# The streamed first weight read through ScalarE's queue instead of SyncE's, and placed behind the fold's first copy in the joint sweep

## The chip, the cores and the metric

One core of a Trainium2 chip runs the whole program in one launch. The metric is device time in microseconds (us) for one execution. TensorE (PE) multiplies, VectorE (DVE) and ScalarE (ACT) do the element work, GpSimd (POOL) does a little of it, and SyncE (SP) only issues transfers. A transfer can be issued by more than one engine: each has a queue of its own, and an engine issues in program order, so an instruction that waits holds everything behind it in that engine's queue.

## The reference

Eight heads of attention with 32 packed positions, then a mix over the sequence, then a mix over channels:

```python
p_packed = sm_attn(p, k, v)              # (8, 8, 32, 64)
out = sm_attn(q, p_packed, p_packed)     # (8, 8, 576, 64)
x = out.transpose(0, 2, 1, 3).reshape(8, 576, 512)
u = x + (x.transpose(0, 2, 1) @ U @ V).transpose(0, 2, 1)
result = u + np.maximum(u @ w_ch1, 0.0) @ w_ch2   # w_ch1 512x2048, w_ch2 2048x512
```

`sm_attn` scales, subtracts the row maximum, exponentiates, divides by the sum, and multiplies with the values. All data are float32.

## The kernel before, in words

**The fold.** The output of attention is a weighted sum of 32 packed rows, so `u @ w_ch1` need not be multiplied with the whole 512 rows of the weight for every position. For each batch the kernel first multiplies the packed rows with the weight. This is the fold: `fold_products` (L556 to 563) takes a quarter of the columns of `w_ch1`, a tile of 128 x 2048 float32 (1 MB), and writes two PSUM banks with eight matmuls (L562, `t_ps`). `folded` (L565 to 576) then splits each bank into a high half, copied by ScalarE (L574, `wth`), and a low half, the difference, made by VectorE (L576, `wtl`). There are four casts of each kind per quarter. A float32 product is then three matmuls: high with high, low with high, high with low (L100, L101, L102 into `h_ps`).

**The quarters.** The four quarters c = 0 to 3 are folded once for each of the eight batches. For the first two batches they lie on chip as `w1t[c]`; while they are there, each is also saved to DRAM (`save_w1`, L549, tensor `w1D`). From then on the room is wanted for other tiles, and each quarter is read back from `w1D` when it is needed, into one tile `w1s` with a single buffer (`stream_w1`, L552 to 554). So a read of the next quarter cannot start before the eight matmuls of the quarter before have read the tile, and the next eight matmuls cannot start before the read has landed. There are 24 such reads: two in the loop of the second batch (at `kt` 10 and 14, L1275 to 1278), and the rest in the six late batches.

**The rest.** Each half of a first product leaves PSUM through ScalarE (`leave`, L1034: into `bits`, `ppall` and others; `last1`, L801: into `aP`). The second product with `w_ch2` is done by sweeps over eight turns (`Sweep.turn`, L1085, into four banks `o`), with seven products in place of eight for a 2 x 2 block, so sums of operands are formed first by VectorE (L1046 to 1048), split high by ScalarE (L1069) and low by VectorE (L1074). Of the sums of `w_ch2` some are brought from DRAM, 256 KB at a time (`bring`, L952, `tc<-tD`). Part of the hidden values of each batch is held out to DRAM (L1037, `hD`; L979, `hjD`) and read back later. Each batch's packed rows are loaded by L958 and L966, the queries by L290, the packed values for the fold by L137, and results are stored by L849.

**The order.** Nothing is scheduled by the hardware or by a planner: the order of instructions on each engine is the order in which the Python program calls them, and that is written out by hand as strings of short words. `run` (L1392 to 1406) goes through the words; each names a list of calls in the table `stages` (L1349 to 1388) and takes the next call from it. `batch_steps` holds one late batch, `joint_steps` (L1315 to 1319) what follows the first four batches, and `last_steps` the end. The words that matter here, with or without a closing `n`, `j` or `J`: `F0` the fold's eight matmuls, `F1` one high cast, `F2` one low cast, `S` one call of `stream_w1`, `H` one half of a first product, `E` the eviction of a half, `L` a cast of `last1`, `G` products of a sweep's turn, `C` and `D` the high and low split, `P` one `bring`, `W` one store of held-out values, `M` and `N` emptying and combining the sums of a sweep, `O` a store of results, `Y` and `Z` the save and the reload of rows.

In `batch_steps` every `S` already stands directly behind the first `F1` after its `F0`, or some words later; in `joint_steps` the one `Sn` stands near the end of the second line, after `Wn G`. `joint_steps` is run once, behind batch 3.

**Semaphores.** The program's transfers signal their landing on a small set of semaphores that are used in turn, and a later transfer on the same semaphore waits for the earlier one.

Of the kernel before, what the change touches and what calls it, by code (L numbers as in the profile page):

```python
# [20 lines left out]
def packed_attention_mixer_kernel(  # L21
# [27 lines left out]
    nc = tc.nc  # L49
    B, H, S, D = q.shape  # L50
# [20 lines left out]
    U, V, w1, w2 = (a.bitcast(I32) for a in (U, V, w1, w2))  # L71
# [53 lines left out]
    w1D = [dram.tile([P, 4 * QW], F32, name=f"w1D{c}", tag=f"w1D{c}") for c in range(NPC)]  # L125
# [425 lines left out]

    def stream_w1(c):  # L552
        t = w1t["s"] = pipe.tile([P, 4, QW], F32, name="w1s", tag=f"w1t{NPC - 1}", bufs=1)
        nc.sync.dma_start(out=t.rearrange("p x n -> p (x n)"), in_=w1D[c])

    def fold_products(b, c):  # L556
        f_ps = [bank() for _ in range(2)]
# [702 lines left out]
    for kt in range(NK):  # L1260
# [11 lines left out]
        if kt % 4 == 2:  # L1272
            n = NPC + kt // 4 + 1
            fold(n // NPC, n % NPC)
            if kt == 10:  # L1275
                stream_w1(0)
            if kt == 14:
                stream_w1(1)
# [8 lines left out]
        c, y = divmod(kt - 1, 2)  # L1287
# [26 lines left out]
    )  # L1314
    joint_steps = (  # L1315
# [3 lines left out]
    )  # L1319

# [55 lines left out]
    for x in ("", "n"):  # L1376
        stages.update({
            "H" + x: [lambda h=h: h[0].half(*h[1:]) for h in halves[x]],
            "E" + x: [lambda h=h: h[0].leave(*h[1:]) for h in halves[x]],
            "L" + x: [lambda h=h: h[0].now.last1(2 * h[1] + h[2]) for h in halves[x] if not h[0].r and h[2] < 2],  # L1380
            "W" + x: [lambda h=h: h[0].hold_out(h[1]) for h in halves[x] if h[2] == 3],
            "F0" + x: [lambda f=f: fold_one(NPC * f[0] + f[1]) for f in folds[x]],
            "F1" + x: [lambda f=f, m=m: folded_one(4 * (NPC * f[0] + f[1]) + m, False) for f in folds[x] for m in range(4)],
            "F2" + x: [lambda f=f, m=m: folded_one(4 * (NPC * f[0] + f[1]) + m, True) for f in folds[x] for m in range(4)],
            "S" + x: [lambda f=f: stream_w1((f[1] + 1) % NPC) for f in folds[x] if f != (B - 1, 3)],
        })
# [52 lines left out]
```

## Time and profile before

| | us |
|---|---|
| median of 3 runs (764.04, 764.5, 764.6) | 764.5 |
| profiled execution, its own time | 765.2 |
| span of the profiled execution | 763.2 |
| TensorE busy in the span | 749.9 |
| VectorE busy | 587.5 |
| ScalarE busy | 405.7 |
| GpSimd busy | 84.9 |

The granted clock of TensorE is 1.0, the upper of its two levels, over the whole span. The profile is one execution, read with its own span as the measure; the median of the other runs is 0.7 us below its own time.

In the rows below a line such as L562 is a line of the kernel, `t_ps<-w1s,ppT` says which tile is written from which, and x16 means sixteen instructions in a row taken together. A bracket at the end of a timeline's row gives the idle time of the engine just before it and what ended it. `SPq` and `ACTq` are the sequencers of SyncE and ScalarE, which issue transfers; the duration of a transfer's row there is that of the issue, not of the transfer. In a chain of waits a row that begins with DMA is the transfer itself, from issue to landing.

### The profile page before, as it was taken

How to read it: one execution, taken by the hardware profiler on the slowest of the kernel's cores; microseconds unless marked ns; L12 is line 12 of the kernel's file. 1: busy time of each engine (PE TensorE's matmuls, PEld its weight loads, DVE VectorE, ACT ScalarE, POOL GpSimd, SP SyncE). 2: the span in 40 equal slices, each digit the busy share in tenths (PEclk: the TensorE clock that was granted, in tenths of full speed). 3: DMA queues.
4: the chain of work that ended last, by engine and by line, in shares of the span. 5: the costliest groups of instructions: out<-in, count | busy, mean ns of one | idle time of the engine just before them, and what ended most of it. 6: DMA issues, size and time to landing. Idle time of an engine off the chain costs nothing.

```text
span 763.2 us, 19553 instructions
## 1 busy us (share of the span) xinstructions
PE 749.9 (98%) x7795; PEld 662.2 (87%) x7795; DVE 587.5 (77%) x1216; ACT 405.7 (53%) x1018; POOL 84.9 (11%) x116
## 2 busy tenths in 40 slices
PE   8999999999999999999999999999999999999997
PEld 6667787887878889998999989999999989999997
DVE  4799789976787768867888768867887678764876
ACT  4788765554343645555455544555554554555451
POOL 1123111010111002100201002010201020200000
PEclk9999999999999999999999999999999999999999
DMA  9999984369112874656478474657464746463672
GB/s 318 337 355 305 324 219 157 112 228 300 40 42 88 254 250 140 221 195 200 130 229 267 132 245 148 185 168 244 145 192 166 253 126 202 148 239 125 198 224 105
DMA packets 106090, 151.78 MB, mean 199 GB/s; under 512 B 40464, under 2 KB 60176, under 8 KB 102416
## 3 DMA queue, kind: packets, MB, share of 16 engines
q1 hardware_dynamic: 105856, 150.28, 61.6%
q8 instruction: 62, 1.02, 0.5%
q14 instruction: 28, 0.23, 0.1%
q10 hardware_dynamic: 144, 0.26, 0.1%
HBM read 116.56 MB, written 33.95 MB: 197 GB/s over the span
## 4 chain that ended last, share of the span: by engine, by line
PE 85%; DMA 6%; DVE 4%; ACT 3%; issue 1%; SPq 0%; POOL 0%; ACTq 0%
PE o L1085 33%; PE h_ps L100 9%; PE h_ps L101 8%; PE h_ps L102 8%; PE t_ps L562 4%; PE o L100 3%; PE o L101 3%; PE o L102 3%; DMA w1s<-w1D 2%; DMA kx<-in_k_dram 2%; PE t_ps L301 1%; PE o L1114 1%; PE s_ps L321 1%; PE t_ps L321 1%; PE m_ps L696 1%
## 5 line engine op out<-in xcount | busy, mean ns | idle before, releaser
L1085 PE MATMUL o<-w2h,h 128*128 128x256 f32 x832 | 166.9, 281 | 0.0
L100 PE MATMUL h_ps<-ah,wth 128*128 128x256 f32 (+1 forms) x512 | 157.5, 308 | 0.6 <-ACT hj L801 0.3
L101 PE MATMUL h_ps<-al,wth 128*128 128x256 f32 (+1 forms) x512 | 150.4, 294 | 0.0
L102 PE MATMUL h_ps<-ah,wtl 128*128 128x256 f32 (+1 forms) x512 | 150.3, 294 | 0.0
L1085 PEld LDWEIGHTS o<-w2h,h 128*128 128x128 f32 x832 | 136.2, 189 | 2.6 <-issue 2.6
L1074 DVE TENSOR_TENSOR h<-bits,h 128x896 fp32r<-128x896 f32 (+1 forms) x104 | 107.8, 1037 | 31.2 <-ACT h L1069 30.5
L1069 ACT CAST h<-bits 128x896 fp32r<-128x896 f32 (+1 forms) x104 | 93.7, 901 | 58.0 <-DVE bits L1048 39.7
L100 PEld LDWEIGHTS h_ps<-ah,wth 128*128 128x128 f32 x512 | 96.4, 188 | 25.2 <-ACT ppall L1034 8.4
L1085 PE MATMUL o<-w2l,h 128*128 128x256 f32 x416 | 116.0, 279 | 0.0
L101 PEld LDWEIGHTS h_ps<-al,wth 128*128 128x128 f32 x512 | 96.3, 188 | 1.0
L102 PEld LDWEIGHTS h_ps<-ah,wtl 128*128 128x128 f32 x512 | 96.3, 188 | 0.0
L1034 ACT ACTIVATE bits<-h_ps 128x256 f32<-128x256 f32 x132 | 49.5, 385 | 67.4 <-PE h_ps L102 51.5
L1085 PE MATMUL o<-tb,h 128*128 128x256 f32 x468 | 81.2, 282 | 0.1
L1085 PEld LDWEIGHTS o<-w2l,h 128*128 128x128 f32 x416 | 78.1, 188 | 0.0
L576 DVE TENSOR_TENSOR wtl<-t_ps,wth 128x256 fp32r<-128x256 f32 x128 | 49.4, 417 | 29.4 <-ACT wth L574 28.3
L1085 PEld LDWEIGHTS o<-tb,h 128*128 128x128 f32 x468 | 66.7, 189 | 0.6 <-DVE h L1074 0.3
L1046 DVE TENSOR_TENSOR bits<-bits 128x256 f32<-128x256 f32 x96 | 42.9, 447 | 28.6 <-ACT bits L1034 28.4
L574 ACT CAST wth<-t_ps 128x256 fp32r<-128x256 f32 x128 | 42.6, 376 | 27.0 <-PE t_ps L562 20.4
L452 POOL TENSOR_TENSOR al<-aT,ah 128x320 fp32r<-128x320 f32 (+1 forms) x32 | 31.4, 985 | 207.0 <-ACT ah L448 178.4
L100 PE MATMUL o<-w2h,h 128*128 128x512 f32 x128 | 52.1, 407 | 0.0
L101 PE MATMUL o<-w2l,h 128*128 128x512 f32 x128 | 50.6, 395 | 0.0
L102 PE MATMUL o<-w2h,h 128*128 128x512 f32 x128 | 50.5, 395 | 0.0
(212 smaller groups left out, 1379.8 us busy)
## 6 DMA issues: line engine op xcount, KB each, us to landing
w1s<-w1D SPq DMA_DIRECT2D x24, 1024.0 KB, 5.5
tc<-tD SPq DMA_DIRECT2D x94, 256.0 KB, 3.1
bits<-in_moe_w_ch_dram SPq DMA_DIRECT2D x32, 512.0 KB, 4.6
kx<-in_k_dram SPq DMA_DIRECT2D x16, 576.0 KB, 5.9
x<-in_q_dram SPq DMA_DIRECT2D x16, 576.0 KB, 5.9
out_dram<-os SPq DMA_DIRECT2D x33, 256.0 KB, 2.9
vt<-in_v_dram SPq DMA_DIRECT2D x32, 256.0 KB, 6.1
hD<-ppall SPq DMA_DIRECT2D x30, 256.0 KB, 4.1
```

The costliest lines, as they stand in the source:

```text
L100: nc.tensor.matmul(ps, lhsT=lh, rhs=rh, start=start, stop=False)
L101: nc.tensor.matmul(ps, lhsT=lh, rhs=rl, start=False, stop=False)
L102: nc.tensor.matmul(ps, lhsT=ll, rhs=rh, start=False, stop=stop)
L452: nc.gpsimd.tensor_tensor(al, aT[:, ns], ah.bitcast(F32), op=ALU.subtract)
L562: nc.tensor.matmul(f_ps[g][xs], lhsT=ppT[b][zs, g, xs], rhs=w[zs, h // 2], start=True, stop=True)
L574: nc.scalar.copy(hi[:, g], src)
L576: nc.vector.tensor_tensor(lo[:, g], src, hi[:, g].bitcast(F32), op=ALU.subtract)
L1034: nc.scalar.activation(dst[:, 256 * (i % 2):256 * (i % 2) + 256], src, AF.Relu)
L1046: vec(l[:, 4:6], s[:, 1:3], s[:, 0:1].to_broadcast([P, 2, P]), op=ALU.add)
L1069: nc.scalar.copy(h[:, ks], src)
L1074: nc.vector.tensor_tensor(lo[:, ks], src, h[:, ks].bitcast(F32), op=ALU.subtract)
L1085: nc.tensor.matmul(ps, lhsT=a, rhs=b, start=x not in self.begun, stop=last and i == 2)
```

## The change

Two edits. `stream_w1` issues its transfer on ScalarE's queue instead of SyncE's, in all of its 24 calls; and in `joint_steps` the word `Sn` moves from behind `Wn G` to directly behind the first `F1n`, so that there too the read stands right after the fold's first high cast. Nothing is computed differently, and no transfer is added or left out.

```diff
     def stream_w1(c):
         t = w1t["s"] = pipe.tile([P, 4, QW], F32, name="w1s", tag=f"w1t{NPC - 1}", bufs=1)
-        nc.sync.dma_start(out=t.rearrange("p x n -> p (x n)"), in_=w1D[c])
+        nc.scalar.dma_start(out=t.rearrange("p x n -> p (x n)"), in_=w1D[c])
@@ joint_steps
-        "Ln PJ D G F0n C N A N N D G O G G U En F1n G F1n G C G G En U Hn N Hn En N Hn D O En Pn Hn Ln Pn En Wn G Sn "
+        "Ln PJ D G F0n C N A N N D G O G G U En F1n Sn G F1n G C G G En U Hn N Hn En N Hn D O En Pn Hn Ln Pn En Wn G "
         "G C G Mv F1n G D En Ln M G Yn M Zn U Hn M F2n Hn En F2n F2n En F1n F2n Wn "
```

## Rows read from the trace of the kernel before

**Rows 1.** The page, part 1: busy time, share of the span, instructions.
```profile
PE 749.9 (98%) x7795; PEld 662.2 (87%) x7795; DVE 587.5 (77%) x1216; ACT 405.7 (53%) x1018; POOL 84.9 (11%) x116
```
**Rows 2.** TensorE's waits: line, releaser, us in total, times, longest.
```profile
PE t_ps L562 <- DMA w1s<-w1D: 1.4, 2, 0.9
```
**Rows 3.** TensorE's timeline: start, us, instruction, idle before and what ended it.
```profile
279.89 1.09 PE L562 MATMUL t_ps<-w1s,ppT 64*32 64x512 f32 x16 [0.92 <-DMA w1s<-w1D]
...
446.21 1.09 PE L562 MATMUL t_ps<-w1s,ppT 64*32 64x512 f32 x16 [0.49 <-DMA w1s<-w1D]
```
**Rows 4.** The page, parts 3 and 6: queues; issues with KB, median us to landing.
```profile
q10 hardware_dynamic: 144, 0.26, 0.1%
...
w1s<-w1D SPq DMA_DIRECT2D x24, 1024.0 KB, 5.5
tc<-tD SPq DMA_DIRECT2D x94, 256.0 KB, 3.1
```
**Rows 5.** Chains of waits, from 268 to 282 and 430 to 448 us.
```profile
273.39 6.37 DMA w1s<-w1D
...
437.31 8.76 DMA w1s<-w1D
```
**Rows 6.** ScalarE's timeline, 267 to 277 us.
```profile
269.15 0.65 ACT L574 CAST wth<-t_ps 128x256 fp32r<-128x256 f32 x2 [0.64 <-PE t_ps L562]
...
271.56 0.67 ACT L1034 ACTIVATE bits<-h_ps 128x256 f32<-128x256 f32 x2
...
274.92 0.38 ACT L1034 ACTIVATE ppall<-h_ps 128x256 f32<-128x256 f32 x1 [2.57 <-PE h_ps L102]
```
**Rows 7.** SyncE's timeline, 335 to 346 us, and its waits (as rows 2).
```profile
335.70 0.46 SPq L554 DMA_DIRECT2D w1s<-w1D  x1
...
339.49 5.51 SPq L966 DMA_DIRECT2D ppP<-ppD  x4
...
SPq L966 <- DMA w1s<-w1D: 12.7, 5, 3.0
```
**Rows 8.** Line 958 around 266.8 us: issues with durations in ns; landing times.
```profile
L958 SPq DMA_DIRECT2D aP<-aD x2: 486/830/1175, 265.6 to 266.8; - x2
...
DMA to landing us min/median/max: 5.0/5.6/6.1
```
**Rows 9.** TensorE's timeline, 273 to 275 us.
```profile
273.95 0.37 PE L100 MATMUL h_ps<-ah,wth 128*128 128x256 f32 x1
```
**Rows 10.** Timelines of SyncE, 425 to 440 us, and ScalarE, 427 to 432 us.
```profile
426.14 7.91 SPq L849 DMA_DIRECT2D out_dram<-os  x2
...
427.63 0.64 ACT L574 CAST wth<-t_ps 128x256 fp32r<-128x256 f32 x2
430.26 0.52 ACT L1069 CAST h<-aJ 128x384 fp32r<-128x384 f32 x1 [2.00 <-PE o L1085]
```
**Rows 11.** Line 554: its issues, ns min/median/max, first and last start.
```profile
L554 SPq DMA_DIRECT2D w1s<-w1D x24: 320/424/715, 226.3 to 681.6; - x24
```
**Rows 12.** Line 1069's wait (ns, as rows 11) and ScalarE's timeline there.
```profile
L1069 ACTq EVENT_SEMAPHORE  x1: 1672/1672/1672, 317.0 to 317.0; - x1
...
317.02 0.66 ACT L1034 ACTIVATE bits<-h_ps 128x256 f32<-128x256 f32 x2 [0.26 <-DVE h L1074]
```
**Rows 13.** Line 952 at 317.1: issue, landing; TensorE's timeline where it is used.
```profile
L952 SPq DMA_DIRECT2D tc<-tD x1: 537/537/537, 317.1 to 317.1; - x1
...
DMA to landing us min/median/max: 2.8/2.8/2.8
...
321.62 0.52 PE L1085 MATMUL o<-tc,h 128*128 128x256 f32 x3
```
**Rows 14.** ScalarE's timeline, 315 to 318.5 us.
```profile
315.76 0.64 ACT L574 CAST wth<-t_ps 128x256 fp32r<-128x256 f32 x2
```
**Rows 15.** Chains of waits, 329 to 333 and 506 to 510 us: TensorE's products.
```profile
329.75 3.07 PE o L1085 x27
...
506.66 3.18 PE o L1085 x27
```

## The prediction

> **What bounds the kernel now.** I read the page first: TensorE is busy for 98% of the span [rows 1], so only time in which it stands still, or is made to stand still, can change the end. Next, whom TensorE waited for: behind the opening stages two of its waits are worth naming, and both are for the streamed first weight, 1.4 us together, the longest 0.9 [rows 2]. Its timeline shows where: the fold's products at 279.89 stood 0.92 us and those at 446.21 stood 0.49 us, each released by the read's landing [rows 3]. The reads themselves are 1 MB each, 24 of them, median 5.5 us from issue to landing, and all of them leave through SyncE's queue, in line with 94 reads of 256 KB (L952) and the rest; ScalarE's queue carried 0.26 MB in the whole run [rows 4]. So what the change can give directly is those two waits, 0.92 + 0.49 = 1.4 us, which is 0.18%. I count 0.2%, 1.5 us, as about what a measurement of this kernel tells from no change.
>
> The profiled execution took 765.2 us, 2.0 more than its span of 763.2, and lies 0.7 above the median of 764.5. The sum is made on the span, and its difference is carried to the median.
>
> **Part 1: the read behind the products at 279.89.** The chain of waits from 268 to 282 us goes from ScalarE through SyncE's store and its save of hidden rows (L979, 272.69) to the read at 273.39, which lands 6.37 later [rows 5]. On ScalarE's queue the read stands directly behind its cast at 269.15 [rows 6], so it no longer waits for that save. But it cannot leave at once. SyncE's queue shows that a transfer waits for the landing of the one eight places ahead: the four reads at 339.49 take 5.51 us to issue because the third of them stands eight behind the weight's read at 335.70 (one L1037 and four L958 lie between), and L966 waits for that read in five places, 12.7 us in total [rows 7]. I take this counter to be common to both queues, since the trace has only the one transfer on ScalarE's and can't show it. Eight ahead of the read at 273.39 (one L979, two L849, four L966 between) is the last L958, the second of a pair issued at 265.6 and 266.8; their landing times are 5.0 and 6.1 us [rows 8]. Taking the shorter for the later one, it lands at about 266.8 + 5.0 = 271.8. The read then leaves at 271.9, not 273.39: 1.5 us earlier, more than the 0.92 that TensorE waited. Gain: 0.9 us.
>
> The price is that ScalarE stands still from 269.2 to 271.9 with the read at its head, 2.3 us or so beyond the 0.2 to 0.4 it has free. Queued behind it are the fold's three other casts, the cast for VectorE's low part and the evictions L1034 at 271.56. ScalarE has 2.57 us idle before 274.92 [rows 6], so it catches up, but TensorE needs the banks those evictions free for its next half at 273.95 [rows 9]. The two evictions end at 272.24; 2.3 later is 274.5, so TensorE stands up to 0.6 us; if the first eviction alone decides, about 0.3. Bounds 0 and 0.8; I take 0.4, between these.
>
> **Part 2: the joint sweep's read.** SyncE issued it at 437.31 [rows 5] behind two stores that held the queue from 426.14 for 7.91 us; ScalarE does the fold's first copies at 427.63 [rows 10] and then has 2.00 us idle, so the issue costs nothing there. The read leaves some 9 us earlier and is down long before TensorE came for it at 446.21 - 0.49 = 445.7 [rows 3], even if it takes the 8.8 us that it took. Gain: 0.5 us. Nothing is next late: the products are then ready 9 us ahead.
>
> **Part 3: the 22 other issues on ScalarE.** One such issue took 320 to 715 ns on SyncE, median 424 [rows 11]. The read's own wait, for the fold's products, has ended when ScalarE gets there: the cast in front of it waited for them. I cost them at nothing, because the queue works ahead of the engine: a wait of L1069 that belongs to the next instruction begins at 317.0 and lasts 1.67 us, while the engine is executing the eviction that began at 317.02 [rows 12]. An issue of 0.42 that starts with a cast of 0.38 leaves a hole of about 0.1. If that cover fails, each read pushes ScalarE by 0.42, 10.1 us in 24; ScalarE has gaps of 0.2 to 2 us every few instructions, so nearly all of it is taken up, and I bound it by one place per batch that has none: 6 x 0.42 = 2.5 us. From below a gain is excluded, as nothing is taken off ScalarE.
>
> **Part 4: the transfers that no longer stand in one line.** SyncE's queue loses 24 issues (10 us) and 25 us of waiting in front of them, so that what stands behind the reads leaves earlier; TensorE waits for none of that. But what stands ahead of them may now be met by them. In five sweeps the read L952 of 256 KB is the last transfer before the weight's read. At 317.1 it lands 2.8 us later, at 319.9, and TensorE uses it at 321.62: 1.7 us to spare [rows 13]. ScalarE reaches its place with the casts at 315.76 [rows 14], so the 1 MB read would go out ahead. The difference of the median landings, 5.5 - 3.1 = 2.4 us [rows 4], is what the small one can lose by it. The other four, by the same three rows of each: 1.8 to spare at 655.11, 0.3 at 498.62 (there it took 5.0 us), and 2.4 at two more. At a full 2.4 that is 0.7 + 0.6 + 2.1 + 0 + 0 = 3.4 us; at none it is 0. No row of this trace shows two busy queues beside each other. I take 0.6, one of the two middling places, since the transfers' sum of bytes is the same and the read needs its own microsecond to begin.
>
> First what the row shows: the read at 273.39 landed after 6.37 us in a queue that still held stores [rows 5]. The Trainium skill, "DMA: Bandwidth & Descriptors", section "Queues, rings and completion order", says that SyncE and ScalarE each own a row and that every DMA engine goes round among the rows that have work, packet by packet. By that rule the weight's read overtakes the queue, which is the slower rival below. The same page, "Issuing engines are not separate DMA queues", adds that issuing from two engines saves only the issuer's time; by it the sum would be without Part 1's gain.
>
> **Sum.** -0.9 + 0.4 - 0.5 + 0 + 0.6 = -0.4: 764.5 - 0.4 = **764.1 us**. TensorE's own pace is left as it is, and adds to the range: 27 products of L1085 took 3.07 us at 329.75 and 3.18 at 506.66 [rows 15] at the same granted clock, and which of the two holds changes at places I can't predict; but whole batches differ by only some 0.15, so I allow 0.6 either way.
>
> **Rivals.**
> - *Faster: both waits go and nothing comes back.* Parts 1's price and 4 at zero: -1.4, and with the pace in favour -2.0: 762.5. For it: the small reads of Part 4 lie in gaps of 1.7 and more. Against: ScalarE's stop at 269 is in the order of the transfers.
> - *Slower: the 1 MB read overtakes the small one.* As Part 4 at its full price: -0.9 + 0.4 - 0.5 + 3.4 = +2.4: 766.9. It decides from a delay of 1.7 us on. For it: ScalarE does get there first at 317 and 650. Against: only three places are tight. The Trainium skill's round among the rows, cited above, is on its side.
> - *Slower: the issue isn't covered on ScalarE.* -0.4 + 2.5 = +2.1: 766.6.
> - *The change moves nothing.* If the read at 269 leaves ScalarE no earlier than SyncE sent it, Part 1 is only price: +0.4 - 0.5 + 0.6: 765.0, within 0.2%.
>
> **How the numbers follow.** Forecast 0.48, nothing moved 0.08, faster 0.20, overtaken 0.17, not covered 0.07. So within 0.2% 0.56, faster 0.20, slower 0.24. The range goes from the faster rival, which has the pace in its favour, 762.5, to the overtaken one with the pace against it, 766.9 + 0.6 = 767.5; about one in ten is left out on each side.
>
> **What would show it.** Right: TensorE's waits for w1s gone from the list; a ScalarE idle of about 2.3 us near 269.5, and none like it elsewhere; ScalarE's queue carrying 24 MB and the joint's read leaving near 428. Wrong: waits of TensorE for tc near 321, 498 and 655 (overtaken); gaps of 0.4 us on ScalarE behind each read, with TensorE waiting for h_ps (not covered); the read near 272 not leaving before 273 (nothing moved). Above all a common counter that holds ScalarE in more places than the one at 269 would make the forecast too low.

## The result

The changed kernel took 773.6 us (median of four runs, 771.4 to 774.6) against 764.3 us (median of four runs): slower by 1.2%, a ratio of 1.0118 with a 95% interval of 1.0095 to 1.0140, or some 9 us. The forecast was 764.1, and the range ended at 767.5.

The page of the changed kernel, parts 1, 3 and 6, answers to [rows 1] and [rows 4]:

```profile
span 771.1 us, 19564 instructions
...
PE 751.9 (98%) x7795; PEld 661.8 (86%) x7795; DVE 588.7 (76%) x1216; ACT 406.5 (53%) x1018; POOL 84.6 (11%) x116
...
q1 hardware_dynamic: 102400, 125.11, 51.4%
q10 hardware_dynamic: 3600, 25.43, 9.6%
...
w1s<-w1D ACTq DMA_DIRECT2D x24, 1024.0 KB, 5.7
tc<-tD SPq DMA_DIRECT2D x94, 256.0 KB, 2.9
```

25 MB have gone from the first queue to the second, as intended. The median landings have hardly moved (5.7 for 5.5, 2.9 for 3.1), and TensorE's busy time is 2 us longer; neither row gives away 9 us. TensorE's waits do (columns as in [rows 2]):

```profile
PE o L1085 <- DMA tc<-tD: 3.4, 3, 1.3
...
PE t_ps L301 <- DMA x<-in_q_dram: 1.3, 1, 1.3
PE t_ps L562 <- DMA w1s<-w1D: 1.3, 1, 1.3
```

Before, the last of these came to 1.4 in two places ([rows 2]), and the other two were not among the waits of 0.2 us or more. Where they are, by TensorE's timeline; the second and the fourth row answer to [rows 3], the third to [rows 13]:

```profile
271.43 1.09 PE L562 MATMUL t_ps<-w1s,ppT 64*32 64x512 f32 x16 [1.31 <-DMA w1s<-w1D]
282.32 1.09 PE L562 MATMUL t_ps<-w1s,ppT 64*32 64x512 f32 x16
325.16 0.62 PE L1085 MATMUL o<-tc,h 128*128 128x256 f32 x3 [1.00 <-DMA tc<-tD]
449.93 1.09 PE L562 MATMUL t_ps<-w1s,ppT 64*32 64x512 f32 x16
503.66 0.61 PE L1085 MATMUL o<-tc,h 128*128 128x256 f32 x3 [1.06 <-DMA tc<-tD]
526.38 0.63 PE L301 MATMUL t_ps<-ident,x 128*128 128x128 f32 x4 [1.33 <-DMA x<-in_q_dram]
663.13 0.62 PE L1085 MATMUL o<-tc,h 128*128 128x256 f32 x3 [1.34 <-DMA tc<-tD]
```

Both old waits are gone, and five new ones have come, all for transfers. TensorE's instructions are the same 7795 in the same order in both kernels, so each can be set beside its counterpart by number. The steps by which the changed kernel (called after from here on) falls behind at one instruction are, in us: 1.4 at 271, then -1.0 at 282, 1.1 at 325, -0.6 at 450, 1.3 at 504, 1.5 at 526, 1.6 at 663. Two more parts are small: 0.9 between 230 and 265 us, and 0.6 in many little ones. From 230 to 700 us that is 6.8. Another 1.1 has gathered by 140 us, ahead of the first streamed read, where nothing was edited, and the tail adds nothing: 7.9, the difference of the two spans.

What happened to a transfer, by line, beside its counterpart. First the `tc` read at 319.3 in after ([rows 13] has it before, 2.8 us to landing):

```profile
L952 SPq DMA_DIRECT2D tc<-tD x1: 536/536/536, 319.3 to 319.3; - x1
...
  PE o L1085: 1.0, 1
...
DMA to landing us min/median/max: 5.8/5.8/5.8
```

Then the queries' read (L290) of before, at 511.6, and of after, at 516.8:

```profile
L290 SPq DMA_DIRECT2D x<-in_q_dram x1: 551/551/551, 511.6 to 511.6; - x1
...
DMA to landing us min/median/max: 6.0/6.0/6.0
```

```profile
L290 SPq DMA_DIRECT2D x<-in_q_dram x1: 583/583/583, 516.8 to 516.8; - x1
...
DMA to landing us min/median/max: 9.4/9.4/9.4
```

And the weight's third read, at 262.6 in after; before, at 260.7, it took 6.0 us:

```profile
L554 ACTq DMA_DIRECT2D w1s<-w1D x1: 327/327/327, 262.6 to 262.6; - x1
...
  PE t_ps L562: 1.3, 1
...
DMA to landing us min/median/max: 8.7/8.7/8.7
```

So the damage runs both ways: small transfers beside the read land 1.5 to 3.4 us later, and the read itself is stretched by 2.7 us, with a store of SyncE's (L849, at 262.87) just behind it. How the two queues share the engines is seen from 500 to 502 us of after, while the `tc` read issued at 497.1 is still out. The view of the transfers has queue, pieces (packets in the view), MB and share of 16 engines:

```profile
q10 hardware_dynamic: 89, 0.72, 90.4%
q1 hardware_dynamic: 11, 0.02, 3.5%
```

In these 2 us the weight's queue moved 89 pieces of 8 KB and SyncE's queue 11 small ones. One piece of the weight costs 0.904 x 16 x 2 / 89 = 0.325 us of an engine. Its 128 pieces are 8 to an engine if they are spread evenly, so by this estimate an engine that has turned to the weight is away for about 8 x 0.325 = 2.6 us, and a `tc` read with a few pieces left on such an engine waits for it. No view names the engine of a piece, so this is worked out and not seen. The Trainium skill, "DMA: Bandwidth & Descriptors", section "Queues, rings and completion order", states that an engine drains a whole packet, typically 9 to 17 descriptors, from one queue before it goes on to the next. The trace agrees as far as it goes: 89 pieces of the weight pass with 11 small ones among them; where a packet ends no view shows.

### The profile page after: what moved, and what is told of

Read it like the earlier page. It is cut to its first block, busy times and chain, and to the rows that moved or that the text cites. A ratio compares the mean times of both kernels' runs of the same rounds, so it can differ in the third digit from the quotient of the medians.

```text
span 771.1 us, 19564 instructions
## 1 busy us (share of the span) xinstructions
PE 751.9 (98%) x7795; PEld 661.8 (86%) x7795; DVE 588.7 (76%) x1216; ACT 406.5 (53%) x1018; POOL 84.6 (11%) x116
## 4 chain that ended last, share of the span: by engine, by line
PE 76%; DMA 10%; DVE 7%; ACT 4%; issue 1%; SPq 1%; POOL 0%; ACTq 0%; DVEq 0%
PE o L1085 30%; PE h_ps L100 8%; PE h_ps L101 7%; PE h_ps L102 7%; PE t_ps L562 4%; DMA bits<-in_moe_w_ch_dram 3%; PE o L100 3%; PE o L101 3%; PE o L102 3%; DMA tc<-tD 2%; PE t_ps L301 1%; DMA kx<-in_k_dram 1%; PE o L1114 1%; DMA x<-in_q_dram 1%; PE t_ps L321 1%
```

## Experiments

Two theories were set against each other. A: the two queues share the 16 transfer engines, so that what used to be served in order of issue is now served side by side, and what TensorE needs first lands late. B: ScalarE, standing at 24 issues and at their semaphores, holds up the evictions. The ratio is to executions of the kernel before that were measured alongside; their medians were 765.6 to 766.1 us, so that times which an expectation counts from 764.3 lie some 1.5 us low. "230 to 700" is how much longer TensorE took from the instruction that the first trace of before ran at 230.2 us to the one that it ran at 700.1, worked out from one timeline each; it leaves out the opening, which is in no kernel's edits and varied by 0 to 2.2 us.

| run | ratio, 95% interval | 230 to 700, us |
|---|---|---|
| before, three traces | | 0, -1.3, -0.6 |
| after, three traces | 1.0118 (1.0095 to 1.0140) | +6.8, +7.9, +8.6 |
| e1_move_only | 0.9998 (0.9985 to 1.0010) | -0.2 |
| e2_queue_only | 1.0119 (1.0096 to 1.0141) | +8.6 |
| e3_two_on_act | 1.0008 (0.9996 to 1.0019) | -1.1 |
| e4_19_on_act | 1.0034 (1.0011 to 1.0057) | +1.5 |
| e5_small_on_act | 0.9998 (0.9986 to 1.0010) | -0.7 |
| e6_2kb_pieces | 1.0053 (1.0032 to 1.0073) | +1.4 |
| e7_gpsimd | 1.0060 (1.0040 to 1.0080) | +4.4 |
| e8_five_on_act | 1.0093 (1.0063 to 1.0123) | +3.0 |
| e10_2kb_one_queue | 1.0013 (1.0003 to 1.0022) | -0.2 |
| e11_later | 1.0125 (1.0075 to 1.0176) | +9.5 |
| f1_behind_casts, two traces | 1.0032 (1.0013 to 1.0052) | -0.5, +0.9 |
| f2_both_behind, two traces | 1.0004 (0.9987 to 1.0021) | -1.3, +2.5 |

### The two parts alone

e1_move_only keeps `nc.sync` and moves the word; e2_queue_only keeps the word's place and changes the queue.

```diff
-... U En F1n G F1n G C ... Wn G Sn "
+... U En F1n Sn G F1n G C ... Wn G "
```

> Only the joint sweep's one read is moved behind the fold's first copy; all 24 reads stay on SyncE's queue. Theory A (two queues share the transfer engines, so the 1 MB reads stretch the small transfers and are stretched by them): with one queue nothing is shared, so only the 0.5 us wait at 446 goes: 763.8, between 763.4 and 764.5. Rival B (the loss is ScalarE standing at its issues and their semaphores): the same. Rival C (the moved word itself costs, since the read now stands ahead of two stores): over 766.

> All 24 reads on ScalarE's queue, the joint sweep's word left where it was. Theory A: as the changed kernel plus the 0.5 us wait at 446 that comes back, 774, between 772.5 and 775.5, with TensorE waiting for tc near 324, 503 and 663 and for the queries near 526. Rival B: the same time. Rival C: near 765.

The move costs nothing, and the queue makes the whole loss. In e2 the expected wait at 446 did not come back, although the read stood at its old place; the row answers to the second of [rows 3]:

```profile
452.02 1.09 PE L562 MATMUL t_ps<-w1s,ppT 64*32 64x512 f32 x16
```

So theory A's figure for that wait was wrong in e2. Its absence there says little of the edit: further down, two of three traces of the kernel before do not have the wait either.

### Some reads on ScalarE's queue, some on SyncE's

`stream_w1` counts its calls and takes ScalarE's queue for some of them; the word is moved in all three kernels.

```diff
+    reads = []
 ...
+        reads.append(c)
+        queue = nc.scalar if len(reads) - 1 in (3, 10) else nc.sync
-        nc.sync.dma_start(...)
+        queue.dma_start(...)
```

> Only the reads behind the two waits of before (the 4th, near 272, and the joint sweep's, the 11th) go through ScalarE's queue, the others through SyncE's; the joint word is moved. Theory A: both waits go and no tight transfer is met: 764.3 - 0.9 - 0.5 = 762.9, between 762.3 and 763.9. Rival B: ScalarE stands for a semaphore at the 4th read and costs 0.4 or more there: 763.3 to 764.3.

> As the changed kernel, but the five reads next to which TensorE's new waits stand (the 3rd, 6th, 14th, 15th and 22nd, at 263, 319, 498, 516 and 657 us of after) go back to SyncE's queue; 19 stay on ScalarE's. Theory A: the new waits of 1.4, 1.1, 1.3, 1.5 and 1.6 us go, 6.9 together: 773.6 - 6.9 = 766.7, between 765 and 768. Rival B (cost by the number of issues on ScalarE): 19/24 of the loss stays, 764.3 + 7.4 = 771.7.

> Only the five reads of the fourth experiment's list (3rd, 6th, 14th, 15th, 22nd) go through ScalarE's queue, the other 19 through SyncE's, joint word moved. Theory A: behind the opening the five bring the 5.4 us that the fourth experiment took away, less the joint's 0.5: 764.3 + 4.9 = 769.2, between 768 and 771, with waits for tc at 324, 503 and 663. Rival B (by the number of issues): 5/24 of 9 us: 766.2.

The five reads that stand beside the new waits carry the loss: without them 19 issues on ScalarE cost 2.6 us (e4), with them alone it is 7.1 us (e8). By number of issues it would have been the other way round. The 7.1 us are more than the 4.9 that theory A gave, and no trace shows them in full: the one execution that was profiled is, with 769.5 us, the shortest of e8's five, and the three longest had a lower mean granted clock (0.995 to 0.998, against 1.0). Its waits:

```profile
PE t_ps L566 <- DMA w1s<-w1D: 2.1, 1, 2.1
PE o L1089 <- DMA tc<-tD: 1.6, 4, 0.7
```

e3 is level with before and not 1.4 us better. It does show ScalarE's stop at the common semaphores, as Part 1 foretold, on ScalarE's timeline (`ACTq` is its queue's issue; two added lines shift the numbers by 4):

```profile
271.10 0.37 ACT L578 CAST wth<-t_ps 128x256 fp32r<-128x256 f32 x1 [0.64 <-PE t_ps L566]
273.54 0.35 ACTq L558 DMA_DIRECT2D w1s<-w1D  x1
273.94 0.65 ACT L578 CAST wth<-t_ps 128x256 fp32r<-128x256 f32 x2 [2.46 <-DMA ppP<-ppD]
```

ScalarE stands for 2.46 us at a transfer of SyncE's queue. Then TensorE's timeline of e3:

```profile
276.46 0.39 PE L100 MATMUL h_ps<-ah,wth 128*128 128x256 f32 x1
```

TensorE ran this matmul at 273.95 before ([rows 9]); in e3 it was 1.95 us behind up to 273, and is 2.5 behind here. So the stop cost TensorE 0.6 us. e4 has the same stop: ScalarE stood 3.02 us until 274.01, and TensorE fell 1.1 us behind there, a good part of what e4 still loses. In the changed kernel the same place cost nothing: TensorE had been held up by the read ahead, the semaphores had come free, and ScalarE stood for 0.33 us.

### Issues without bytes

e5_small_on_act leaves the 24 reads on SyncE's queue, with the word moved, and lets ScalarE issue a transfer of 64 bytes at each of the 24 places.

```diff
+    spot = dram.tile([1, 16], F32, name="spot")
         nc.sync.dma_start(out=t.rearrange("p x n -> p (x n)"), in_=w1D[c])
+        nc.scalar.dma_start(out=spot, in_=w1D[c][:1, :16])
```

> All 24 reads stay on SyncE's queue (joint word moved); at each of the 24 places ScalarE's queue issues in addition one transfer of 64 bytes from the weight to a spare place in DRAM, which takes part in the round of semaphores and moves next to no bytes. Theory A (shared transfer engines): nothing of the loss comes, apart from ScalarE's stop at the 4th place, 0.5 us: 764 to 765.5, no new waits of TensorE for tc. Rival B (ScalarE's issues and semaphore waits): most of the 9 us comes: 769 to 773.

The small transfers by their line (durations in ns, first and last start):

```profile
L557 ACTq DMA_DIRECT2D spot<-w1D x24: 475/475/561, 228.8 to 682.4; - x24
```

24 issues of 0.475 us each on ScalarE, in the same round of semaphores, cost nothing: 0.9998. ScalarE did stand 1.74 us here at the 4th place, until 272.9, and TensorE lost nothing by it; in the changed kernel it stood for no more than 0.33 us behind any of its 24 reads. So theory B falls as the cause of the loss, though a stop at a semaphore can cost something, as e3 and e4 show.

### The size of a piece

e6_2kb_pieces lays the saved weight out in DRAM so that a read goes in pieces of 2 KB; e10_2kb_one_queue does the same on SyncE's queue.

```diff
-    w1D = [dram.tile([P, 4 * QW], ...
+    w1D = [dram.tile([4 * P, QW], ...
 ...  (save_w1 likewise)
-        nc.scalar.dma_start(out=t.rearrange("p x n -> p (x n)"), in_=w1D[c])
+        nc.scalar.dma_start(out=t, in_=w1D[c].rearrange("(x p) n -> p x n", p=P))
```

> As the changed kernel, but the saved weight lies in DRAM so that each read (and each of the four saves) goes in pieces of 2 KB instead of 8 KB; bytes, queue and places are the same. Theory A1 (the engines serve the two queues piece by piece, so a queue with 8 KB pieces gets four times the share of one with 2 KB pieces): TensorE's waits for tc near 324, 503 and 663 (4.0 together) shrink to under 1.5 together, the weight's reads take longer, the wait near 271 grows by up to 1: 770, between 768 and 772. Theory A2 (shares don't depend on the size of a piece): the waits for tc stay, 772 to 775.

> Pieces of 2 KB as in the sixth experiment, but all reads on SyncE's queue (joint word moved): the size of a piece alone. Theory A1 (8 KB pieces hurt the small transfers only where two queues alternate): on one queue the size is worth nothing, a ratio to before of 0.998 to 1.003. Rival D (small pieces are faster in themselves): the 4 us by which the sixth experiment was better than the changed kernel come here too, a ratio of 0.995 or less.

e6's waits of TensorE:

```profile
PE o L1085 <- DMA tc<-tD: 1.0, 2, 0.8
...
PE t_ps L301 <- DMA x<-in_q_dram: 0.7, 1, 0.7
```

The waits for `tc` fall to 1.0, from 3.1 to 5.2 in three traces of the changed kernel, and half of the loss is gone, while the weight's reads take longer (median 6.5 us). On one queue the smaller piece helps nothing (1.0013). So small pieces are worth something only where there are two queues. The expected growth of the wait near 271 was a miss: in this trace it was absent, which is a part of the gain.

A1's reason, that the engines serve the two queues piece by piece, does not hold as a rule. From 497.75 to 499.5 us of e6 a `tc` read issued at 495.9 was still out (it landed at 501.5), and yet the weight's queue moved 322 pieces of 2 KB in a row and SyncE's queue none, which has no row in the view:

```profile
q10 hardware_dynamic: 322, 0.66, 99.9%
```

That is some 20 pieces to an engine, if they are spread evenly. The `tc` read issued just ahead of the weight's, at 494.2, landed at 497.9, as that stretch began. Why the smaller piece takes half of the loss away stays open.

### Another queue

e7_gpsimd issues the reads on GpSimd's queue instead of ScalarE's.

> As the changed kernel with the reads on GpSimd's queue in place of ScalarE's: a second queue too, but ScalarE issues nothing and the semaphores are not those of SyncE's round. Theory A: the same kind of waits come back (tc 3 to 5 us together, the queries, the weight near 271): 769 to 775. Rival B: with ScalarE free the loss goes: 763.5 to 765.5.

TensorE's waits of e7:

```profile
PE t_ps L329 <- DVE x L412: 2.2, 4, 0.8
PE t_ps L562 <- DMA w1s<-w1D: 1.8, 1, 1.8
```

The time is in theory A's interval, and the stretched read near 271 is there, but the waits for `tc` are not (0.4 in all), and 2.2 us of waiting for VectorE are new. ScalarE being free did not bring the loss down to nothing (two executions), which is against B; why this queue harms VectorE's work rather than `tc` was not followed up and stays open.

### Moving the read away from what it meets

e11_later puts `S` two turns later in `batch_steps`, f1_behind_casts puts it behind the fold's third high cast, and f2_both_behind moves the `Sn` beside the queries behind the next fold's first cast as well.

```diff
 e11  -... F2 E Rj S G U E G F2 H C P Plj U H D G F1 F1 G F2 E ...
      +... F2 E Rj G U E S G F2 H C P Plj U H D G F1 F1 G F2 E ...
 f1   +... F2 E Rj G U E G F2 H C P Plj U H D G F1 F1 S G F2 E ...
 f2   also: -... D a0 Hn Sn Pj Rj Rj Hn En Wn Pj Ln Hn Ln F1n G F1n En ...
            +... D a0 Hn Pj Rj Rj Hn En Wn Pj Ln Hn Ln F1n Sn G F1n En ...
```

> As the changed kernel, but the third weight's read of each batch is issued two turns of products (6 us) later on ScalarE, when the L952 read beside it has landed; queue, pieces and bytes are unchanged. Theory A: the three waits for tc (4.0 us together) go, the rest stays: 773.6 - 4.0 = 769.6, a ratio to before of 1.004 to 1.009. Rival E (the read delays what is needed wherever it lies): waits of the same size for other transfers, a ratio of 1.011 or more.

> As the changed kernel, but the third weight's read of each batch is issued behind the fold's third high cast instead of its first, some 3 us later on ScalarE, when the L952 read beside it has landed. Queue, pieces and bytes are unchanged. Theory A (order and overlap): TensorE's waits for tc near 324, 503 and 663, 4.0 us together, go: a ratio to before of 1.003 to 1.009. Rival E (the read delays what is needed wherever it lies): waits of the same size elsewhere, 1.010 or more.

> As the run before, and also the read beside the queries and packed values (near 516 us) goes behind the fold's next casts, some 3.7 us later, so that the queries' read is no longer overtaken. Theory A: the wait near 526 (1.5 us) goes as well, the one near 271 (1.4 to 1.8) stays: a ratio to before of 1.000 to 1.005. Rival E: 1.010 or more.

e11 tells nothing about the order, since the read did not move: ScalarE waits for nothing in those two turns, and issued it at 320.18, after an eviction that began at 320.17; the `tc` read was issued at 320.33. Its waits for `tc` stayed (4.2 us in five).

f1 does move it: the first of the three leaves at 320.54, 2.5 us behind the start of the `tc` issues at 318.06. The waits for `tc` are gone in both of its traces, and TensorE's products run without one:

```profile
322.36 0.52 PE L1085 MATMUL o<-tc,h 128*128 128x256 f32 x3
```

With that the loss falls from 1.2% to 0.3%. In f2 the queries' wait goes too, and the kernel is level with before (1.0004), with all 24 reads on the second queue. The same bytes, queue and pieces cost 9 us or nothing, by what is in flight beside them. f2 has a price of its own in its second trace, where a read that leaves later lands 1.15 us late for its products at 585.46.

### Second and third traces

> The kernel before once more. In the eight traces since, TensorE reaches the instruction that it ran at 230 us between 0.1 and 2.2 us later, though nothing that lies ahead of it was edited. Theory N (the opening varies by itself): this run too shows 0.5 to 2 us there and nothing behind it: 764.3 to 767. Rival O (a second queue in use delays the opening): 0 within 0.3 at 230 us.

> The kernel before for a third trace. Theory A: the waits for the weight at 280 and 446 are no fixed property of the kernel, since the reads' landing differs by 1 us from run to run: at least one of the two is absent or under 0.3 us. Rival (they are, and the second trace was the exception): 0.9 and 0.5 again, within 0.2.

> The changed kernel once more, for how much its own waits vary. Theory A: the waits at the same places (weight near 271, tc near 324, 503, 663), each within 0.7 us of the first trace; the place at 526 (queries) may differ by more, since the order of two issues 0.4 us apart decides it. Rival N (chance): other places.

> The changed kernel for a third trace. Theory V: the read near 262 us may take 6 or 9 us. Rival K: 8.5 to 9.5. The waits for tc near 324, 503 and 663 come again, at least two of the three over 0.5 us.

The kernel before, second trace and third trace, at the two places of [rows 3]:

```profile
278.93 1.09 PE L562 MATMUL t_ps<-w1s,ppT 64*32 64x512 f32 x16
445.09 1.09 PE L562 MATMUL t_ps<-w1s,ppT 64*32 64x512 f32 x16
```

```profile
280.72 1.09 PE L562 MATMUL t_ps<-w1s,ppT 64*32 64x512 f32 x16 [0.64 <-DMA w1s<-w1D]
```

The second has neither wait, and its own time is 763.7; the third has 0.64 at the first place and none at the second, and one of 0.56 us for `tc` at 727, so such a read can be late on a single queue too. The opening gave 0 in the second and 1.1 in the third, in the same kernel, and 0.1 to 1.1 in three traces of after: it varies by itself (theory N), though not in the run that was meant to show it. The changed kernel's waits come again: for `tc` 3.1 us in two places in its second trace (325 and 663, none at 503), and by the list of waits of its third

```profile
PE o L1085 <- DMA tc<-tD: 5.2, 4, 2.2
PE t_ps L562 <- DMA w1s<-w1D: 1.6, 1, 1.6
```

with one at 403 that the other two do not have and none at 324. Most of the places repeat, the sizes do not.

A part of the third trace's loss is the clock. TensorE stood 2.19 us for `tc` there, and from 504.7 to 508.1 us its granted clock (the third figure from the right in the second row) was 0.5, the lower of its two levels, 1.2 GHz:

```profile
504.20 0.62 PE L1085 MATMUL o<-tc,h 128*128 128x256 f32 x3 [2.19 <-DMA tc<-tD]
504.70:508.10 3.40, 3.40 (x18) 3.40 (x18) 2.40 (x4) 0.69 (x2) 1.41 (x1) 0.50 0.32 84
```

The 18 matmuls from 504.65 on took 3.65 us, against 2.11 in the first trace of after: 1.5 us on top of the wait. e11 has the same behind its wait of 1.66 us at 584.89 (0.51 from 585.3 to 588.8, again 1.5 us). The first two traces of after and e2, with waits of up to 1.8 us, have no such fall. So 1.5 us of the +8.6 of the third trace and of e11's +9.5 followed a wait and were none. Some of the longest executions without a trace also have a lower mean clock (774.1 and 774.6 us of after at 0.998, 773.9 of e4 at 0.995); what it cost there was not traced.

> The same kernel as f1_behind_casts once more, for the read near 262 us. Theory V (it varies from execution to execution): 8.5 to 9.5 us in this run or in the next, with a wait of TensorE of 1.3 to 2 behind it. Rival K (it belongs to the kernel): 6.0 to 6.3 in both, and no wait. The waits for tc stay away in either case.

> The same kernel as f2_both_behind once more. Theory V: the read near 262 us takes 8.5 to 9.5 us in this run or the one before it. Rival K: 6.0 to 6.3. No waits for tc or the queries in either case, and a time within 2 us of the kernel before.

The third read, from issue to landing, in the two traces of f1_behind_casts:

```profile
L554 ACTq DMA_DIRECT2D w1s<-w1D x1: 326/326/326, 262.4 to 262.4; - x1
...
DMA to landing us min/median/max: 6.0/6.0/6.0
```

```profile
L554 ACTq DMA_DIRECT2D w1s<-w1D x1: 342/342/342, 261.6 to 261.6; - x1
...
  PE t_ps L562: 1.4, 1
...
DMA to landing us min/median/max: 8.7/8.7/8.7
```

Same kernel, same transfers around it, 6.0 or 8.7 us. In f2 it is 6.1 and 8.7. So theory V holds: on two queues the outcome is drawn anew in each execution. The store behind the read does not decide it alone: it was issued 0.25 us behind the read in f1's first trace (6.0) and in f2's second (8.7). The time of f2's second trace was a miss: 768.5 us, expected within 2 us of the kernel before, whose one execution beside it took 763.1. The changed kernel drew 8.7 to 9.1 in all three traces.

## Why the prediction was wrong

**The step that failed is Part 4's price.** It named the right mechanism, and among its five places the three where TensorE then waited, and took 0.6 us where these three alone cost 4.0 (1.1, 1.3 and 1.6). The reason given, that the sum of the bytes is the same and the read needs its own microsecond to begin, does not touch what the row from 500 to 502 us points to: not the mean rate counts, but the last pieces of the small transfer, held up while the weight's pass. The weight's read does need such a time (its first piece came 1.0 to 1.4 us behind its issue in the five reads beside the new waits, first trace of after), and the small transfers were late all the same. The bound of 2.4 us per place, from the difference of the median landings, was nearly right: `tc` landed 3.0 us later at 319, 1.5 at 497 and 3.3 at 657. "The 1 MB read overtakes the small one" was the true rival, and 0.17 was too little for it.

**What Part 4 left out.** It asked only which `tc` read stands ahead of the weight's read. The same sharing hits every transfer in flight, whichever was issued first: the queries' read (3.4 us later, 1.5 us of TensorE), and the weight's own read, stretched from 6.0 to 8.7 us with a store behind it (1.4 us). A store of the sums at 251.4 landed in 5.1 us instead of 2.8, so ScalarE waited for it. That lies in the 0.9 before 265, but no run took it alone. "What stands behind the reads leaves earlier; TensorE waits for none of that" was true of leaving and false of landing. That is why the measured time lies above even that rival's 766.9.

**Part 1's gain was priced from one execution.** The row was read rightly, and the wait did go. But it is 0.9, 0 and 0.6 us in three traces of the kernel before, so about 0.5 on average and not 0.9. Part 2's is 0.5, 0 and 0: the joint read's mechanism is right (it left at 431.75 and TensorE no longer waits), and it is worth some 0.2. The sign was there to be seen: the profiled execution lay 0.7 above the median.

**Part 1's price and the semaphores** were right in kind where the case arose: 2.46 and 3.02 us of standing in e3 and e4 against 2.3, and 0.6 and 1.1 us of TensorE against 0.4, the second above the bound of 0.8. That the size in e3 is so near is in part luck: by the profile ScalarE stood there for a load of `ppP` (L966), and not for the last load of L958 that Part 1 named. In the changed kernel the stop was 0.33 us and cost nothing.

**Part 3** was right: ScalarE's issues cost nothing (e5), so "not covered" falls. "Moves nothing", at 765.0, falls by the measured time.

**The range** allowed 0.6 us for TensorE's pace and nothing for the opening, which varied by 0 to 2.2 us. That is second to the 6.3 us that Part 4 missed (4.0, 1.5 and 1.4, less its 0.6). It also had no term for the clock, which took 1.5 us in the third trace.

No version here beats the kernel before: e1, e3, e5 and f2 are level with it. In e3 the 0.6 us at ScalarE's stop are set against what the two waits can give, 1.4 us by the first trace of before, 0 and 0.6 by the other two.

## What to carry to other kernels

Moving a large transfer to a second queue takes away the order between it and every other transfer. List what is in flight from its issue to its landing, on either side of it, and set each one's slack against the time that one engine needs for its whole share of the large one (here 8 pieces of 0.325 us, 2.6 us). Where the slack is smaller, issue the large one later (that took the whole loss away here), or in smaller pieces (half of it), or leave it in line. And price a wait only after a second trace has shown it again: these two, 1.4 us together, were absent from the next execution.

## What the runs showed of the hardware

- The program's common round of semaphores ties ScalarE's queue to SyncE's: ScalarE stood 2.46 us (e3) and 3.02 us (e4) for a transfer that SyncE had issued.
- The size of a piece mattered between two queues and not within one: 2 KB instead of 8 KB brought the ratio from 1.0118 to 1.0053 on two queues and gave 1.0013 on one.
- Sharing between two queues is not the same from run to run: one read, issued at the same place among the same transfers, took 6.0 or 8.7 us.
- The two queues do not always take turns piece by piece: 322 pieces of 2 KB of one queue passed in 1.75 us while a transfer of the other was out (e6).
- A wait of TensorE can cost its clock as well: behind waits of 2.19 and 1.66 us the granted clock was 0.5 for some 3.5 us, 1.5 us more each time (third trace of the changed kernel, e11).
